# Asking for the inputs of units 8 to 11 as soon as their buffers are free

## The chip, the cores and the metric

One core of a Trainium2 chip runs the kernel. The metric is device time in microseconds (us); of several executions the median is given. Beside it stands one execution that was taken with the profiler.

## What is computed

The kernel joins a gated scan over 4 sequences of 3648 tokens (256 channels) with a two-level mixture of experts: a router picks one of 4 groups and one of 4 experts in it for each of the 14592 tokens, so one of 16 experts, each a two-layer network of 256 to 1024 to 256.

```
sig = 1 / (1 + exp(-f_logit));  f = lower_bound + (1 - lower_bound) * sig
for t in range(S):  h = f[:, t] * h + (1 - f[:, t]) * x[:, t];  y[:, t] = h
x = y.reshape(B * S, D)
g = argmax(x @ w_group);  e = argmax(x @ w_expert[g]);  weights g_w, e_w by softmax
out[token] = g_w * e_w * (relu(x[token] @ w1[g, e]) @ w2[g, e])
```

## The kernel before

**Units.** The tokens are cut into 29 units of 512. Each unit's input (gate and x, 1 MB) is fetched by `p1_load` (L178 to L203). Units 4 to 7 land in eight 512 KB staging tiles `st`; all others land in tiles `zt`, of which four exist. So units 0 to 3 take the four, and units 8 to 11 take them again in the same order. Units up to 11 are asked for by SyncE (SP) on its queue, later ones by ScalarE (ACT), L202. A unit then passes tanh (L216) and an affine step (L226) on ScalarE, a gate (L263 or L242) and two scans (L253) on VectorE, a transpose to rows on TensorE (L281) with its copy (L283), the router's matmuls (L300) and the routing on VectorE. GpSimd scatters the rows to per-expert lists in DRAM (`xs`, L390). The last reader of a unit's `zt` is its second scan.

**Jobs.** An expert's rows are worked on as jobs. The first sixteen ("A") begin before all tokens are routed; job n is cut at the unit that `EARLY` names, and `choose` (L644) picks its expert, so that its weights can be fetched. Jobs 0 to 2 are "raw": f32 weights, four pieces of 512 KB straight into tiles `w` (L939), rows into `xr` (L926), first layer L1043 with its evictions to `hh` and `hl` at L1046, second layer L1078 with its eviction at L1109. Later jobs go through `st` (L943) and a split into two 16-bit parts (L951, L953). Rows in front of a list's start are filled from `blank` (L674).

**Order.** SP issues in the order in which the program is written, for the whole kernel. TensorE, VectorE and ScalarE follow the written order only up to the first job's preparation; from there on a planner lays out their order from the program and its dependences. A background queue of steps (`p1_thunks`) carries the units, and jobs run between them. At unit 3 `choose` fetches the weights of job 0 (`fetch_to` at L665). At unit 5 `early_rows(4)` fetches job 0's rows, then unit 8, then the four pieces of job 1, then unit 9. At unit 7 `early_rows(6)` fetches job 1's rows, unit 10, the four pieces of job 2, unit 11:

```python
        if u == EARLY[0][0]:
            p1_load(8)
            fetch_to(pptr[0] + 4)
            p1_load(9)
        if u == EARLY[1][0]:
            p1_load(10)
            fetch_to(pptr[0] + 4)
            p1_load(11)
```

The tanh of unit u + 1 is written into the steps of unit u; that of unit 11 stands in the steps of unit 10, behind the load of unit 12.

Of the kernel before, what the change touches and what calls it, by code (L numbers as in the profile page):

```python
# [44 lines left out]
MT = -(-max(CAPS) // 128)  # L45
QUARTERS = (13, 14, 15)
ZX_SP = 12


@with_exitstack  # L50
def gated_scan_moe(ctx: ExitStack, tc, zx, lower, wroute, wexp, out, S):
# [110 lines left out]
    def unit_range(u):  # L162
        return u * UNIT, min(N, (u + 1) * UNIT)
# [14 lines left out]
    def p1_load(u):  # L178
        if u >= NU or u in loaded:
            return  # L180
        loaded.add(u)
        a, b = unit_range(u)
        w = b - a
        src = zx[u * P:(u + 1) * P, :].rearrange("p (s k w) -> p s k w", s=2, k=KD)
        if u in STAGED:
            halves = []
            for q in range(2):
                t = stg.tile([P, 1024], F32, name="st").rearrange("p (k w) -> p k w", k=KD)
                nc.sync.dma_start(out=t[:, :, 0:w], in_=src[:, q, :, 0:w])
                halves.append(t)  # L190
            units[u] = {"z": halves[0], "x": halves[1]}
            return
        zt = p1.tile([P, 2, KD, UNIT], F32, name="zt", bufs=4)
        if u == 0:
            for k in range(KD):
                for q in range(2):
                    nc.sync.dma_start(out=zt[:, q, k, 0:w], in_=src[:, q, k, 0:w])
        elif u == 1:
            for k in range(KD):
                nc.sync.dma_start(out=zt[:, :, k, 0:w], in_=src[:, :, k, 0:w])  # L200
        else:
            last_load[u] = (nc.sync if u < ZX_SP else nc.scalar).dma_start(out=zt[:, :, :, 0:w], in_=src[:, :, :, 0:w])  # L202
        units[u] = {"z": zt[:, 0], "x": zt[:, 1]}  # L203
# [239 lines left out]
    def p1_thunks(us, groups, parts):  # L443
# [22 lines left out]
        def put(f):  # L466
            th.append(f or (lambda: None))
            if hasattr(f, "mark"):
                marks[f.mark] = len(th)
# [28 lines left out]
        for u in us + [us[-1] + 1]:  # L498
            seq = []
            if u <= FAST:  # L500
                put(lambda u=u: [p1_load(v) for v in range(2, 8 if u < 8 else u + AHEAD)])
                ending = u - 1 in ends
                if not ending:
                    put(lambda u=u: p1_ta(u + 1))
                if u > 0:
                    put(lambda u=u: p1_router(u - 1))
                    put(lambda u=u: logits(u - 1))
                    if u > 1:
                        put(lambda u=u: p1_gate(u))
                put(lambda u=u: p1_tb(u, 0))  # L510
                wave(u, 1)
                if ending:
                    bind, bound, (s1, f4x, s2, f3, f4, s6, f5, s7s) = routing(u - 1)
                    if u - 1 == BEHIND[2]:
                        f4.mark = "ranked"
                    put(bind)
                    if u > BEGIN:
                        back(u - 1)
                    put(lambda u=u: p1_tanh(u + 1))
                    put(s1)  # L520
                    put(f4x)
                    if u > 1 and member[u - 2] == member[u - 1]:
                        back(u - 2)
                    put(s2)
                    put(f3)
                    put(f4)
                    wave(u, 1)
                    put(lambda u=u: p1_affine(u + 1))
                    back(u - 1)
                    put(bound)  # L530
                    put(s6)
                    put(f5)
                    for f in s7s:
                        put(f)
                    wave(u, 1)
                elif u > 7:
                    wave(u, 1)
                    back(u - 1)
                for m in [m for m, v in ROWS_AT.items() if u == v]:
                    f = lambda m=m: early_rows(m)  # L540
                    f.mark = m
                    put(f)
                if u == BEGIN:
                    f = lambda: None
                    f.mark = "first"
                    put(f)
                put(lambda u=u: p1_tb(u, 1))
                wave(u, 1 if u < FAST else 99)
                if u in cuts and u - 1 in ends:
                    put(lambda u=u: place(u))  # L550
                if u - 1 in ends:
                    put(lambda u=u: choose(u))
                if u == FAST:
                    f = lambda: None
                    f.mark = "begun"
                    put(f)
                    for v in [v for v in sorted(cuts) if v <= FAST and v not in ROWS_AT]:
                        f = lambda v=v: early_rows(v)
                        f.mark = v
                        put(f)  # L560
                continue
            if u in us:
                seq += [lambda u=u: (p1_load(u + AHEAD - 1), u + 1 in us and p1_ta(u + 1))]
            if u - 1 in us:
                seq += [lambda u=u: p1_back(u - 1, 0)]
            if u in us:
                seq += [lambda u=u: p1_tb(u, 0)]
            if u - 1 in us:
                seq += [lambda u=u: p1_router(u - 1)]
                seq += [lambda u=u: p1_back(u - 1, 1)]  # L570
            if u in us:
                seq += [lambda u=u: p1_tb(u, 1)]
            if u - 1 in us:
                seq += [lambda u=u: logits(u - 1)]
            for t in seq:
                put(t)
                slot += 1
                for _ in range(1):
                    if not hold:
                        break  # L580
                    f = hold.popleft()
                    if isinstance(f, tuple) and f[0] == "scat":
                        scatq.extend((slot + n, g) for n, g in zip(PACE, f[1]))
                    elif isinstance(f, tuple):
                        lagq.append((slot + LAG, f[1]))
                    else:
                        put(f)
                while scatq and scatq[0][0] <= slot:
                    put(scatq.popleft()[1])
                while lagq and lagq[0][0] <= slot:  # L590
                    put(lagq.popleft()[1])
            if u - 1 in ends:
                grp = ends[u - 1]
                T = sum(unit_range(v)[1] - unit_range(v)[0] for v in grp) // P
                G = {}

                def bind(G=G, first=grp[0]):
                    G.update(cur.pop("G"))
                    G["rows"] = group_rows.pop(first)
                if u <= 13:  # L600
                    s1, f4x, s2, f3, f4, s6, f5, s7s = route_thunks(G, T, True)
                    rs = [s1, s2, f3, f4x, None, f4, s6, f5]
                else:
                    s1, s2, s3, s4, s5, s6, s7s = route_thunks(G, T)
                    rs = [s1, s2, s3, None, None, s4, s5, s6]
                rs.append(("scat", s7s))
                put(bind)
                rs.append(lambda u=u: choose(u))
                if u in cuts:
                    rs.append(lambda u=u: place(u))  # L610
                    f = lambda u=u: early_rows(u)
                    f.mark = u
                    rs.append(("lag", f))
                hold.extend(rs)
# [77 lines left out]
    def early_rows(u):  # L692
        for mac in macros:
            for j in mac:
                if j.kind == "A" and EARLY[j.idx][0] == u and j.idx < NE - 1:
                    job_rows(j)
        ready[0] = True
        if u == EARLY[0][0]:
            p1_load(8)
            fetch_to(pptr[0] + 4)  # L700
            p1_load(9)
        if u == EARLY[1][0]:
            p1_load(10)
            fetch_to(pptr[0] + 4)
            p1_load(11)

    regs = {}
    early_loads = []
# [423 lines left out]
    pptr = [0]  # L1132
# [28 lines left out]
    def fetch_to(n):  # L1161
        while pptr[0] < min(n, len(pieces)):
            j, i = pieces[pptr[0]]
            if j.kind == "A" and j.idx not in picked:
                return
            if j.kind != "A":
                bg_to(marks["order"])
            job_weights(j, i)
            pptr[0] += 1
        if ready[0]:  # L1170
            ready[0] = False
            blanks()
# [158 lines left out]
```

## Time and profile before

| | us |
|---|---|
| median of 3 runs (766.83 to 768.5) | 767.49 |
| the profiled execution, whole | 772.1 |
| its span, first to last instruction | 770.3 |
| TensorE (PE) busy in the span | 720.9 |
| VectorE (DVE) busy | 530.1 |
| ScalarE (ACT) busy | 450.3 |
| mean granted TensorE clock, share of full | 0.983 |

The profiled execution is 0.6% longer than the median, and 1.8 us of it lie outside the span. The rows below show one execution: starts are us from the span's start; "idle before" with an arrow tells how long an engine stood and what released it. PE and DVE are in the page's words TensorE and VectorE, SPq and ACTq the instructions by which SyncE and ScalarE start a transfer. A busy PE is not a PE at its peak.

### The profile page before, as it was taken

The numbers are of one execution on the slowest core, as the hardware profiler recorded it, in microseconds if no ns is written. First come the engines' busy times: TensorE is split into PE (matmuls) and PEld (weight loads), VectorE is DVE, ScalarE is ACT, GpSimd is POOL, SyncE is SP. The second block draws the span as 40 slices with busy tenths as digits, with TensorE's granted clock in tenths as the row PEclk, the third lists the DMA queues.
The fourth block names the chain that finished last, engine by engine and source line by source line (L and its number), as shares of the span: only waits on it lengthen the run. The fifth ranks groups of instructions, "written<-read, shape, count | busy, mean of one in ns | idle before, by whom it ended". The sixth has DMA issues, their size and how long they took to land.

```text
span 770.3 us, 21391 instructions
## 1 busy us (share of the span) xinstructions
PE 720.9 (94%) x8115; PEld 640.5 (83%) x8115; DVE 530.1 (69%) x1155; ACT 450.3 (58%) x824; POOL 294.5 (38%) x273
## 2 busy tenths in 40 slices
PE   3669799999999999999999999999999999999995
PEld 1557587788878888998999889999999999999995
DVE  6997279999999996678647555454653665657652
ACT  6657368879776965555546444444544555556652
POOL 3666145367775564551221122213322232223223
PEclk9969899999999999999999999999999999999998
DMA  8688899898899666377868652334263555566521
GB/s 325 225 276 314 287 291 323 307 366 289 290 328 320 208 200 212 85 202 185 195 175 183 155 138 83 99 102 124 84 148 111 158 141 162 142 189 182 180 78 32
DMA packets 101383, 152.00 MB, mean 197 GB/s; under 512 B 60898, under 2 KB 70913, under 8 KB 98464
## 3 DMA queue, kind: packets, MB, share of 16 engines
q1 hardware_dynamic: 86752, 103.27, 46.7%
q0 software_dynamic: 11408, 30.02, 10.7%
q10 hardware_dynamic: 3120, 17.34, 6.5%
q8 instruction: 64, 1.05, 0.6%
q14 instruction: 39, 0.32, 0.1%
HBM read 112.66 MB, written 38.40 MB: 196 GB/s over the span
## 4 chain that ended last, share of the span: by engine, by line
PE 66%; DVE 13%; DMA 10%; issue 5%; ACT 3%; POOL 2%; SPq 1%; POOLq 0%; DVEq 0%; ACTq 0%
PE ps_m L1097 31%; PE ps_m L1065 7%; PE ps_m L1067 7%; PE ps_m L1066 7%; DMA zt<-in_zx_dram 3%; PE ps_p L1065 3%; PE ps_p L1066 3%; PE ps_p L1067 3%; DVE h L253 3%; DMA xs<-rows,posi 2%; DVE w L953 2%; PE ps_p L281 2%; DVE hl L1071 2%; DMA st<-in_wexp_dram 2%; ACT zt L226 1%
## 5 line engine op out<-in xcount | busy, mean ns | idle before, releaser
L1097 PE MATMUL ps_m<-w,hh 128*128 128x256 bf16 (+7 forms) x2480 | 304.5, 251 | 0.1
L1097 PE MATMUL ps_m<-w,hl 128*128 128x256 f16 (+3 forms) x1240 | 250.3, 251 | 0.0
L1097 PEld LDWEIGHTS <-hh 128*128 128x128 f16 (+4 forms) x2480 | 183.1, 99 | 21.2 <-issue 2.7
L1065 PE MATMUL ps_m<-xh,w 128*128 128x256 f16 (+10 forms) x782 | 187.2, 254 | 5.4 <-DVE hl L1071 5.4
L1066 PE MATMUL ps_m<-xl,w 128*128 128x256 bf16 (+10 forms) x782 | 187.1, 254 | 0.0
L1067 PE MATMUL ps_m<-xh,w 128*128 128x256 f16 (+10 forms) x782 | 187.1, 254 | 0.0
L390 POOL DMA_INDIRECT xs<-rows,posi x114 | 138.0, 1210 | 121.2 <-ACT rows L285 26.1
L953 DVE TENSOR_TENSOR w<-st,w 128x1024 bf16<-128x1024 f32 x116 | 140.0, 1219 | 50.3 <-ACT w L951 50.3
L1111 POOL DMA_INDIRECT out_dram<-o,info x71 | 83.7, 1178 | 233.4 <-ACT o L1109 204.3
L1071 DVE SCALAR_TENSOR_TENSOR hl<-ps_m,hh 128x512 bf16<-128x512 f32 (+9 forms) x166 | 109.8, 667 | 57.8 <-ACT hh L1070 57.5
L1070 ACT ACTIVATE hh<-ps_m 128x512 f16<-128x512 f32 (+9 forms) x166 | 97.4, 588 | 66.2 <-PE ps_m L1067 66.0
L951 ACT CAST w<-st 128x1024 f16<-128x1024 f32 x116 | 120.2, 1051 | 13.3 <-PE ps_m L1097 8.4
L1066 PEld LDWEIGHTS <-w 128*128 128x128 f16 x1088 | 106.4, 98 | 11.6 <-issue 4.6
L1065 PEld LDWEIGHTS <-w 128*128 128x128 f16 x1088 | 106.5, 98 | 8.4 <-issue 1.2
L1067 PEld LDWEIGHTS <-w 128*128 128x128 bf16 x1088 | 106.4, 98 | 7.0 <-issue 0.2
L1097 PEld LDWEIGHTS <-hl 128*128 128x128 bf16 (+3 forms) x1240 | 97.7, 99 | 11.6 <-issue 2.2
L1111 POOL DMA_INDIRECT out_dram<-o,meta x51 | 59.7, 1171 | 107.0 <-ACT o L1109 94.5
L1109 ACT ACTIVATE o<-ps_m,info 128x256 f32<-128x256 f32 (+4 forms) x71 | 31.5, 444 | 75.0 <-PE ps_m L1097 66.9
L1065 PE MATMUL ps_p<-xh,w 128*128 128x256 f16 (+17 forms) x306 | 71.5, 249 | 0.0
L1066 PE MATMUL ps_p<-xl,w 128*128 128x256 bf16 (+17 forms) x306 | 71.5, 249 | 0.0
L1067 PE MATMUL ps_p<-xh,w 128*128 128x256 f16 (+17 forms) x306 | 71.5, 249 | 0.0
L1071 DVE SCALAR_TENSOR_TENSOR hl<-ps_p,hh 128x512 bf16<-128x512 f32 (+13 forms) x65 | 41.8, 644 | 42.4 <-ACT hh L1070 42.1
(179 smaller groups left out, 827.7 us busy)
## 6 DMA issues: line engine op xcount, KB each, us to landing
st<-in_wexp_dram SPq DMA_DIRECT2D x116, 512.0 KB, 6.5
zt<-in_zx_dram ACTq DMA_DIRECT2D x16, 1024.0 KB, 8.0
xs<-blank SPq DMA_DIRECT2D x28, 258.0 KB, 6.0
zt<-in_zx_dram SPq DMA_DIRECT2D x6, 1024.0 KB, 14.4
w<-in_wexp_dram SPq DMA_DIRECT2D x12, 512.0 KB, 12.8
st<-in_zx_dram SPq DMA_DIRECT2D x8, 512.0 KB, 13.6
xr<-xs SPq DMA_DIRECT2D x14, 258.0 KB, 3.2
xs<-rows,posi POOLq DMA_INDIRECT x114, 6.6
```

The source lines that it names most:

```text
L253: sn = nc.vector.tensor_tensor_scan(out=h[:, k, c0 - a:c1 - a], data0=ff[:, k, c0 - a:c1 - a], data1=uu[:, k, c0 - a:c1 - a], initial=init ...
L390: sc = nc.gpsimd.indirect_dma_start(out=xs_v[G["t0"] + t][:, :], out_offset=bass.IndirectOffsetOnAxis(ap=R["posi"][:, t:t + 1], axis=0), i ...
L951: nc.scalar.copy(j.wh[i], j.st[i])
L953: nc.vector.tensor_tensor(out=j.wl[i], in0=j.st[i], in1=j.wh[i], op=ALU.subtract)
L1065: nc.tensor.matmul(po, w1_at(j.wh, k, c), xh[:, k], start=(k == 0), stop=False)
L1066: nc.tensor.matmul(po, w1_at(j.wh, k, c), xl[:, k], start=False, stop=False)
L1067: nc.tensor.matmul(po, w1_at(j.wl, k, c), xh[:, k], start=False, stop=(k == KD - 1))
L1070: eviction[0] = nc.scalar.activation(hi, pv, AF.Relu).ins
L1071: nc.vector.scalar_tensor_tensor(out=j.hl[ch][:, cs[0]:cs[-1] + 1, 0:w], in0=pv, scalar=0.0, in1=hi, op0=ALU.max, op1=ALU.subtract)
L1097: nc.tensor.matmul(pm[i * q:i * q + n, 0:dw], h[ch][:, c, ts], w2_at(w, c)[:, i * dw:(i + 1) * dw], start=(c == 0 and s == 0), stop=(c == ...
L1109: nc.scalar.activation(o[s, 0:dw], pm[s, 0:dw], AF.Copy, scale=lt.bitcast(F32)[s, r, 1:2])
L1111: nc.gpsimd.indirect_dma_start(out=out_v[out_n[0]].rearrange("n (g d) -> (n g) d", g=g), out_offset=bass.IndirectOffsetOnAxis(ap=lt[s, r, ...
```

## The change

Units 8 to 11 are asked for in other places of SP's order. Unit 8 comes with the steps at the head of unit 2, units 9 and 10 with those at the head of unit 3, unit 11 behind unit 3's second scan and ahead of `choose`, which is to say ahead of job 0's weights. The four loads in `early_rows` go away; the two fetches of job weights there stay. Each load still waits for its buffer. Nothing else changes: the same transfers, the same tiles, the same arithmetic.

```diff
+NEXT_AT = {2: (8,), 3: (9, 10)}
+LAST_AT = {3: (11,)}
...
                 put(lambda u=u: [p1_load(v) for v in range(2, 8 if u < 8 else u + AHEAD)])
+                put(lambda u=u: [p1_load(v) for v in NEXT_AT.get(u, ())])
...
                 if u - 1 in ends:
+                    put(lambda u=u: [p1_load(v) for v in LAST_AT.get(u, ())])
                     put(lambda u=u: choose(u))
...
-        if u == EARLY[0][0]:
-            p1_load(8)
+        if u in (EARLY[0][0], EARLY[1][0]):
             fetch_to(pptr[0] + 4)
-            p1_load(9)
-        if u == EARLY[1][0]:
-            p1_load(10)
-            fetch_to(pptr[0] + 4)
-            p1_load(11)
```

## Rows read from the trace of the kernel before

**Rows 1.** The page, part 2: 40 slices of 19.3 us, busy tenths.
```profile
PE   3669799999999999999999999999999999999995
DMA  8688899898899666377868652334263555566521
```

**Rows 2.** Windows: span, PE, PEld, DVE, ACT, POOL busy us (count), clock, DMA share, GB/s.
```profile
80.00:90.00 10.00, 7.11 (x50) 5.58 (x48) 0.00 (x0) 1.02 (x2) 0.97 (x1) 1.00 0.97 370
94.00:96.00 2.00, 2.00 (x8) 1.63 (x7) 1.90 (x2) 1.76 (x5) 0.00 (x0) 0.50 0.34 117
```

**Rows 3.** ScalarE in order of time: start, us, line, instruction, idle before and releaser.
```profile
76.91 0.33 ACTq L202 DMA_DIRECT2D zt<-in_zx_dram  x1
80.80 0.59 ACT L283 COPY rows<-ps_p 128x512 f32<-128x512 f32 x1
...
90.91 1.06 ACT L216 ACTIVATE zt<-zt 128x1024 f32<-128x1024 f32 x1 [9.53 <-DMA zt<-in_zx_dram]
91.87 0.58 ACT L1046 ACTIVATE hh<-ps_m 128x512 f32<-128x512 f32 x1
...
94.38 1.07 ACT L216 ACTIVATE zt<-zt 128x1024 f32<-128x1024 f32 x1
```

**Rows 4.** TensorE in order of time, across the stall.
```profile
86.51 0.59 PE L1043 MATMUL ps_m<-xl,w 128*128 128x256 f32 x2
92.50 1.22 PE L1043 MATMUL ps_m<-xh,w 128*128 128x256 f32 x2 [5.40 <-ACT hh L1046]
...
98.46 0.69 PE L281 MATMUL ps_p<-ident,h 128*128 128x128 f32 x4
```

**Rows 5.** VectorE in order of time, across the stall.
```profile
93.89 1.23 DVE L242 SCALAR_TENSOR_TENSOR zt<-zt 128x1024 f32<-128x1024 f32 x1 [14.43 <-ACT zt L226]
```

**Rows 6.** SP's transfers in order of time.
```profile
5.39 10.42 SPq L189 DMA_DIRECT2D st<-in_zx_dram  x8
33.44 2.35 SPq L939 DMA_DIRECT2D w<-in_wexp_dram  x4
...
47.62 0.37 SPq L202 DMA_DIRECT2D zt<-in_zx_dram  x1
...
66.08 0.91 SPq L926 DMA_DIRECT2D xr<-xs  x2
...
71.09 0.48 SPq L202 DMA_DIRECT2D zt<-in_zx_dram  x1
```

**Rows 7.** Line 202, both queues, 0 to 160 us: time from issue to landing.
```profile
DMA to landing us min/median/max: 6.0/8.2/14.4
```

**Rows 8.** Windows from 24 to 90 us, columns as in the second group.
```profile
24.00:34.00 10.00, 7.25 (x63) 5.24 (x56) 8.91 (x25) 6.41 (x15) 8.00 (x7) 1.00 0.45 166
34.00:44.00 10.00, 5.68 (x54) 4.62 (x54) 8.82 (x31) 4.72 (x12) 5.72 (x5) 1.00 0.89 281
44.00:48.00 4.00, 3.15 (x29) 2.25 (x28) 3.79 (x12) 2.78 (x7) 0.98 (x2) 0.50 0.17 58
48.00:67.00 19.00, 15.96 (x116) 13.14 (x117) 16.51 (x52) 12.61 (x30) 11.78 (x11) 0.75 0.91 308
```

**Rows 9.** VectorE in order of time: second scan of unit 3.
```profile
29.12 1.25 DVE L253 TENSOR_TENSOR_SCAN h<-zt,h 128x512 f32<-128x512 f32 x1
```

**Rows 10.** TensorE in order of time: job 0's first matmuls, job 1's row transposes.
```profile
57.38 0.82 PE L1043 MATMUL ps_m<-xh,w 128*128 128x256 f32 x2
...
69.07 0.36 PE L1009 MATMUL ps_p<-ident,xr 128*128 128x128 f32 x1 [0.94 <-DMA xr<-xs]
69.70 0.63 PE L1009 MATMUL ps_p<-ident,xr 128*128 128x128 f32 x3 [0.28 <-DMA xr<-xs]
```

**Rows 11.** Windows from 100 to 300 us, and the sum of all four.
```profile
100.00:130.00 30.00, 28.45 (x210) 23.59 (x209) 23.45 (x62) 21.53 (x44) 15.83 (x14) 1.00 0.94 341
130.00:160.00 30.00, 27.18 (x295) 23.44 (x294) 29.72 (x62) 22.69 (x42) 14.52 (x12) 1.00 0.91 309
...
sum 200.00, PE 191.96 PEld 167.20 DVE 185.76 ACT 152.97 POOL 121.42; mean PE 47.99 PEld 41.80 DVE 46.44 ACT 38.24 POOL 30.36
```

## The prediction, made blind
> **What bounds the kernel now.** I began with the page's forty slices [rows 1]. From the sixth slice on TensorE is at 9 tenths nearly throughout, with one hole in the fifth (77 to 96 us) in which the transfer engines stay at 8; so the end is set by TensorE's work, and only time that TensorE loses can be won. The windows show the hole: from 80 to 90 us VectorE does nothing, ScalarE is busy 1.02 us, and the transfer share is 0.97 [rows 2]. A whole core waits for data.
>
> For what, ScalarE's order of time tells. After a row copy at 80.80 it stands 9.53 us until 90.91, released by a `zt` transfer, and then does a tanh [rows 3]. SP's order of time names the transfer: the last `zt` load of SP, unit 11, issued at 71.09 [rows 6]. So 1 MB took 19.8 us, where the loads of this line take 8.2 us in the middle and 14.4 at most among those whose landing is listed [rows 7]. Behind the tanh, in ScalarE's order, stands the eviction of job 1's first layer at 91.87 [rows 3]. TensorE waits for that eviction, 5.40 us, and when it starts at 92.50 it runs at half speed: the two matmuls that take 0.59 us at 86.51 take 1.22 and the granted clock is 0.50, the 1.2 GHz level of the two [rows 2, 4]. VectorE stood 14.43 us for the same unit [rows 5]. This is the only place where the input of a unit holds up all engines.
>
> **What the change removes.** Unit 11 is now asked for as soon as unit 3's second scan ends: that scan starts at 29.12 and takes 1.25, so about 30.5 us instead of 71.09 [rows 6, 9]. Units 8 to 10 go before it. Even at the longest listed landing of 14.4 us [rows 7] unit 11 is there at 45, some 35 us before ScalarE comes to it. The 9.53 us vanish wholly; the working is which part of it TensorE gets.
>
> - TensorE's wait for the eviction: 5.40 us [rows 4].
> - The half clock behind it. From 92.50 to 98.46 TensorE works 5.96 us, at 0.50 [rows 2, 4]. If it hasn't stood, the clock stays at 1.00 as it was until then, and the same work takes half: 3.0 us. Bounds: 0, if TensorE stops elsewhere nearby and the clock falls all the same, and 3.0. I take 3.0, because the busy stretch ahead of the stall ran at full clock.
> - Job 1's rows. TensorE waits 0.94 and 0.28 us for `xr`, issued at 66.08 [rows 6, 10]. SP holds that issue until the scatters have landed, and from 48 to 67 us the transfer engines are at 0.91 with units 8 and 9 and job 1's weights among their load [rows 8]. Without the two units some 2.1 MB are gone from it, 5.7 us of full share at 370 GB/s (166 GB/s at a share of 0.45). I take all 1.2 us; the bounds are 0 and 1.2.
>
> The sum is 5.4 + 3.0 + 1.2 = 9.6 us, with bounds 5.4 and 9.6 from these three terms.
>
> **What it adds: the same four loads, earlier.** No instruction is new; four issues of some 0.4 us each move on SP's queue [rows 6]. Each waits for its buffer, and SP stands meanwhile. Behind them are only the blank rows and job 0's weights, issued at 33.44 [rows 6]; these need `choose`, which comes on VectorE after unit 3's scan, the very thing unit 11's load waits for. So the wait costs nothing and the issue some 0.4 us. SP is free from 15.8 us on, when it has issued the staged halves [rows 6].
>
> What is dearer is what they carry past: 4.19 MB ahead of job 0's weights on one queue. At 370 GB/s that is 11.3 us of all transfer engines. The share is 0.45 from 24 to 34, 0.89 from 34 to 44 and 0.17 from 44 to 48 [rows 8], so 5.5, 1.1 and 3.3 us are free. Job 0's weights are in by about 44 us now, where the share drops. With 11.3 - 5.5 - 1.1 = 4.7 us more ahead they land at about 48.7; if nothing of the free time could be used, at 55.3. Their first matmul starts at 57.38 [rows 10]. Hence nothing is lost, with 2 us to spare in the worst case. The scatters of units 1 to 3 run beside it; their slower landing would hold job 0's row load, which has some 7 us in hand, so 0. In exchange the stretch from 66 to 91 us gets rid of 2.1 MB.
>
> **What is late next.** Once unit 11 is there, ScalarE's next input is unit 12, asked for on its own queue at 76.91 [rows 3]. Its tanh stands at 94.38 now and would stand at about 94.4 - 9.5 - 1.2 = 83.7. With the middle landing of 8.2 us, from 75.7 (the issue moves up by the 1.2), unit 12 is in at 83.9: just in time, 0.2 us or nothing. Job 2's four pieces of weights are the only large load left beside it. From 130 to 160 us VectorE is busy 29.72 of 30 us [rows 11]; it is the bound there, but its own standstill is 14.43 us long [rows 5], so it moves up by no less than TensorE. From 300 us on nothing but TensorE's order counts, and an earlier start is an earlier end.
>
> So 9.6 - 0.1 = 9.5 us. Against the profiled execution that is a span of 760.8 and a whole of 762.6; the median lies 4.6 us under the profile, and 767.49 - 9.5 = **758.0 us**.
>
> **The rivals.**
>
> *Unit 12 takes the place of unit 11.* If its landing takes the 14.4 us of the longest one [rows 7], it arrives at 90.1, and ScalarE stands 6.4 us with the same eviction behind it: 9.5 - 6.4 = 3.1 us remain, 764.4 us. For it: the share is 0.97 now in that window [rows 2]. Against it: unit 11 itself is one of the loads that fill it. There is a rule that bears on this: the Trainium skill, "DMA: Bandwidth & Descriptors", section "Queues, rings and completion order", says that each transfer engine takes turns among the queues that have work for it, a packet from each. By that rule unit 11 lost half its speed when unit 12 started on the other queue, and unit 12 will share with job 2's weights; the trace agrees so far as the 19.8 us go, and the rule pulls toward this rival's 764.4 only if these weights are not yet in at 76.
>
> *The stall is covered by later ones.* Between 100 and 300 us TensorE stands 200 - 192.0 = 8.0 us, with VectorE and the transfers (0.94, 0.91) heavily loaded [rows 11]. If the later pieces of weights and scatters come no earlier, TensorE waits there for what it has won: no change, 767.5. Against it: 4 MB less has to be moved after 48 us. The change not doing what it says falls in here too: SP would have to be held past 60 us.
>
> *The planner's order turns out worse.* Behind job 0's preparation the order of three engines is laid out anew, with unit 11 ready far sooner. If its tanh and scans are put ahead of job evictions, TensorE waits for those. Place: the stretch from 100 to 300 us; price: a scan of 1.25 us [rows 9] for each eviction that falls behind one; point: from 9 such evictions on (9.5 + 1.5 us) the kernel is slower than before. With 16, the price is 20 us and the time 778. For it: VectorE is full there. Against it: the written order and all dependences stay. Job 0's weights being late is no rival of this sign, for they would have to come after 68 us.
>
> *More than the sum.* The 130 to 160 window has 2.8 us of standing TensorE and the one ahead of it 1.6 [rows 11]; with the transfers ahead of their users both could shrink: at most 4.4 us more, 753.6.
>
> **How the numbers follow.** Forecast (755.5 to 761.5): 0.56. More than the sum: 0.10. Unit 12 late, or another part of the 9.5 lost (761.5 to 766): 0.18. No change: 0.09. Worse order: 0.07. The predicted time is the first. The range takes in the first three, and leaves out the last two: 753.0 to 766.0. A measurement of this kernel can tell about 0.2%, 1.5 us, from no change; faster by more than that is 0.84, within it 0.09, slower 0.07.
>
> **What would show it.** SP's order: three `zt` loads between 15.8 and 25 us, one near 30.5, none at 47 to 72. The windows: the share from 24 to 34 near 1, VectorE busy from 80 to 90, no window with a granted clock of 0.50 between 88 and 98. ScalarE: no wait for `zt` of over 2 us behind 60 us; TensorE: the first matmul of job 0 still near 57.4, and the work that stands at 98.46 now near 89. I am wrong if ScalarE stands for unit 12 with evictions behind it, if job 0's first matmul moves, or if TensorE's idle time from 100 to 300 us grows from 8 us by what the stall has lost.

## The result, and the profile after

The changed kernel takes 761.76 us in the median of 6 runs (759.69 to 762.94), beside 768.39 for the kernel before (6 runs, 766.83 to 772.61): a ratio of 0.990, interval 0.988 to 0.992, which is 6 to 9 us. The prediction was 758.0 us, a gain of 9.5; the measured median lies in its range (753.0 to 766.0), but 0.3 us above the forecast's own part of it (755.5 to 761.5), in the part that had a chance of 0.18. The profiled executions stand further apart: 772.1 before and 760.23 after, spans of 770.3 and 758.4, 11.9 us. Lines of the changed kernel below are its own; L204, L218, L924, L937, L941, L1007 and L1107 are the old L202, L216, L926, L939, L943, L1009 and L1109.

The page's slices of the changed kernel answer to [rows 1]:

```profile
PE   3669999999999999999999999999999999999995
DMA  8988899998897854567885752424354455566521
```

TensorE's hole in the fifth slice is filled. Its windows, with the columns of [rows 2] and [rows 8]:

```profile
80.00:90.00 10.00, 10.00 (x88) 8.13 (x88) 6.55 (x15) 8.91 (x20) 0.97 (x1) 1.00 0.73 223
88.00:98.00 10.00, 10.00 (x72) 8.50 (x72) 7.49 (x24) 6.13 (x15) 5.65 (x6) 1.00 1.00 273
...
24.00:34.00 10.00, 7.20 (x63) 5.23 (x56) 8.92 (x25) 6.37 (x15) 7.96 (x7) 1.00 1.03 409
34.00:44.00 10.00, 5.75 (x54) 4.69 (x54) 8.82 (x31) 4.75 (x12) 5.76 (x5) 1.00 1.01 367
44.00:48.00 4.00, 3.16 (x29) 2.24 (x28) 3.79 (x12) 2.76 (x7) 0.98 (x2) 0.51 0.64 252
48.00:67.00 19.00, 15.98 (x114) 12.49 (x115) 17.16 (x51) 15.08 (x33) 11.74 (x11) 0.74 0.69 218
```

VectorE's 0.00 from 80 to 90 has become 6.55, no clock below 1.00 is left between 88 and 98, the transfer share has gone from 0.45 to 1.03 in the 24 to 34 window and from 0.91 to 0.69 between 48 and 67. SP's transfers in order of time, beside [rows 6]:

```profile
16.80 13.92 SPq L204 DMA_DIRECT2D zt<-in_zx_dram  x4
32.71 0.37 SPq L678 DMA_DIRECT2D xs<-blank  x1
33.28 1.98 SPq L937 DMA_DIRECT2D w<-in_wexp_dram  x4
48.31 0.89 SPq L924 DMA_DIRECT2D xr<-xs  x2
...
63.66 0.90 SPq L924 DMA_DIRECT2D xr<-xs  x2
...
82.00 3.56 SPq L924 DMA_DIRECT2D xr<-xs  x4
88.22 1.49 SPq L678 DMA_DIRECT2D xs<-blank  x2
89.97 9.21 SPq L941 DMA_DIRECT2D st<-in_wexp_dram  x7
```

Four loads go out between 16.8 and 30.7 us, job 0's weights at 33.28 instead of 33.44. The rows of job 2 (`xr`, the group of four) are asked for at 82.00; in the kernel before it was 88.76:

```profile
88.76 3.35 SPq L926 DMA_DIRECT2D xr<-xs  x4
93.97 1.46 SPq L674 DMA_DIRECT2D xs<-blank  x2
95.72 27.22 SPq L943 DMA_DIRECT2D st<-in_wexp_dram  x11
```

The prediction did not speak of this line, and the experiments turn on it. What SP waited for ahead of it, between 66 and 90 us, is in the first two lines for the kernel before and in the third for the changed one:

```profile
SPq L926 <- DMA xs<-rows,posi: 8.6, 3, 6.5
SPq L926 <- DMA xs<-blank: 5.9, 1, 5.9
...
SPq L924 <- DMA xs<-rows,posi: 8.8, 3, 7.1
```

(The numbers are the us in total, how often, and the longest.) Job 2's rows can be fetched when the scatters of unit 7 and the blank rows in front of them have landed. In the kernel before the blank rows came last: they are issued behind the four pieces of job 2's weights, land 17.3 us after that, and cost 5.9 us beyond the scatters. In the changed kernel that last wait is gone. From 260 us on the shift between the two kernels does not move any more: the same outputs' evictions on ScalarE start at 271.67 and 714.80 before (first fence), and at 259.78 and 702.92 after (second).

```profile
271.67 0.52 ACT L1109 ACTIVATE o<-ps_m,meta 128x256 f32<-128x256 f32 x1
...
714.80 0.47 ACT L1109 ACTIVATE o<-ps_m,info 128x256 f32<-128x256 f32 x1 [0.49 <-PE ps_m L1097]
```

```profile
259.78 0.52 ACT L1107 ACTIVATE o<-ps_m,meta 128x256 f32<-128x256 f32 x1
...
702.92 0.47 ACT L1107 ACTIVATE o<-ps_m,info 128x256 f32<-128x256 f32 x1 [0.49 <-PE ps_m L1095]
```

So all 11.9 us of the profiled pair arise ahead of the first of these evictions, and none is given back.

### The profile page after: what moved, and what is told of

Its sections match the earlier page's. It is cut to its first block, busy times and chain, and to the rows that moved or that the text cites. A ratio compares the mean times of both kernels' runs of the same rounds, so it can differ in the third digit from the quotient of the medians.

```text
span 758.4 us, 21398 instructions
## 1 busy us (share of the span) xinstructions
PE 718.3 (95%) x8115; PEld 638.5 (84%) x8115; DVE 531.1 (70%) x1155; ACT 450.3 (59%) x824; POOL 296.0 (39%) x273
## 4 chain that ended last, share of the span: by engine, by line
PE 62%; DVE 19%; DMA 8%; issue 4%; ACT 3%; SPq 1%; POOL 1%; POOLq 0%; ACTq 0%; DVEq 0%
PE ps_m L1095 30%; PE ps_m L1063 6%; PE ps_m L1065 6%; PE ps_m L1064 6%; DVE h L255 4%; DVE w L951 4%; PE ps_p L1063 3%; DMA st<-in_wexp_dram 3%; PE ps_p L1065 3%; PE ps_p L1064 3%; DVE hl L1069 3%; DMA xs<-rows,posi 3%; PE ps_p L283 1%; DVE zt L244 1%; ACT w L949 1%
## 5 line engine op out<-in xcount | busy, mean ns | idle before, releaser
L392 POOL DMA_INDIRECT xs<-rows,posi x114 | 141.1, 1238 | 111.3 <-ACT rows L287 25.6
L1109 POOL DMA_INDIRECT out_dram<-o,info x71 | 83.7, 1179 | 233.2 <-ACT o L1107 203.1
L1109 POOL DMA_INDIRECT out_dram<-o,meta x51 | 59.9, 1175 | 104.8 <-ACT o L1107 93.7
L1107 ACT ACTIVATE o<-ps_m,info 128x256 f32<-128x256 f32 (+4 forms) x71 | 31.6, 445 | 73.6 <-PE ps_m L1095 65.8
```

Source lines behind the costliest of these rows:

```text
L392: sc = nc.gpsimd.indirect_dma_start(out=xs_v[G["t0"] + t][:, :], out_offset=bass.IndirectOffsetOnAxis(ap=R["posi"][:, t:t + 1], axis=0), i ...
L1107: nc.scalar.activation(o[s, 0:dw], pm[s, 0:dw], AF.Copy, scale=lt.bitcast(F32)[s, r, 1:2])
L1109: nc.gpsimd.indirect_dma_start(out=out_v[out_n[0]].rearrange("n (g d) -> (n g) d", g=g), out_offset=bass.IndirectOffsetOnAxis(ap=lt[s, r, ...
```

## The experiments

Twelve kernels ran in three groups of four, each group beside the kernel before on one chip. The level differs between the groups: the kernel before took 788.89, 796.3 and 768.97 us there. So ratios to it are compared, and times of different groups are not. Three theories were held: **L**, the gain is unit 11's landing; **T**, it is the 4 MB that leave the crowded stretch; and, formed after the first two groups, **C**, two chains end together near 90 us, unit 11's input and, on SP, job 2's rows with job 3's weights behind them, and both have to come sooner. Line numbers are each kernel's own.

The profiled executions don't all begin alike. Unit 5's tanh stands at 32.3 to 32.7 us in the pair above and in the third group, and at 34.8 to 37.4 in the first two, also in kernels whose moved line comes only later. So starts of a few us apart can't be compared between these, and the third group is the cleanest.

**The kernel before once more (first group).** No edit.

> The kernel before, unchanged, profiled once more. Theory S (the stall for unit 11 is not equally long in every execution, and the profiled one had a long one: its span was 4.6 us over the median's): the wait of ScalarE for unit 11 is shorter here than 9.5 us, some 5 to 7, TensorE's wait 1 to 4 us, and the span shorter by as much. Rival R (the stall is always the same and the executions differ elsewhere, for instance in TensorE's clock or in the stretch from 100 to 270 us): the wait is again 9 to 10 us and TensorE's 5.4, whatever the span is. Time: 767 to 770 us by both.

Ratio 1.0009 (0.998 to 1.004). ScalarE, TensorE and the clock at the stall:

```profile
93.19 1.06 ACT L216 ACTIVATE zt<-zt 128x1024 f32<-128x1024 f32 x1 [7.59 <-DMA zt<-in_zx_dram]
...
94.78 1.22 PE L1043 MATMUL ps_m<-xh,w 128*128 128x256 f32 x2 [3.47 <-ACT hh L1046]
...
94.00:96.00 2.00, 1.22 (x3) 1.04 (x4) 0.00 (x0) 2.00 (x4) 0.00 (x0) 0.59 0.14 49
96.00:98.00 2.00, 2.00 (x9) 1.53 (x8) 1.73 (x2) 1.78 (x5) 0.00 (x0) 0.56 0.04 12
98.00:100.00 2.00, 2.00 (x27) 1.53 (x26) 2.00 (x3) 2.00 (x5) 0.00 (x0) 1.00 0.75 245
```

The stall is there again and smaller: 7.59 instead of 9.53 us on ScalarE, 3.47 instead of 5.40 on TensorE, and the clock is back at 98 us, after some 3.4 us at half, where it stayed low for 6.8 before. Theory S (the text above has it, and its rival R) is right that the stall has no fixed length, and wrong that a shorter one goes with a shorter span: this execution had a span of 795.0 where the median whole time was 790. What the stall cost in the median execution stays open.

**Unit 11 alone in its old place (first group).**

```diff
-LAST_AT = {3: (11,)}
+LAST_AT = {}
...
         if u in (EARLY[0][0], EARLY[1][0]):
             fetch_to(pptr[0] + 4)
+        if u == EARLY[1][0]:
+            p1_load(11)
```

> Units 8, 9 and 10 asked for early as in the change, unit 11 alone in its old place behind job 2's weights. Theory L (the gain is unit 11's landing, and a load asked for at 71 us behind 2 MB of weights lands too late whatever else is gone): ScalarE still waits for unit 11, some 4 to 8 us, and the time is 763.5 to 768. Rival T (the gain is the relief of the transfer engines, 3 of the 4 MB are gone from the crowded stretch): unit 11 lands in some 10 us, the wait is under 2 us and the time 761 to 763.

Ratio 0.9964 (0.993 to 0.999). In this execution ScalarE did not wait for unit 11 at all: it stood for a second-layer matmul until 86.17 and went straight on to the tanh, which by T should have been worth most of the gain. It was not: the time is in L's band, the wait in T's. Job 2's rows were asked for at 89.33, but TensorE does not wait for them: from 72 to 100 us it never stands, and its clock is 1.00. This execution was behind earlier (job 0's first matmul at 62.12, in the kernel before of this group at 57.49), and later ScalarE waits 3.02 us for unit 14's input:

```profile
110.05 1.06 ACT L218 ACTIVATE zt<-zt 128x1024 f32<-128x1024 f32 x1 [3.02 <-DMA zt<-in_zx_dram]
```

Neither theory holds as it was put.

**Unit 11 ahead of job 2's weights (first group).** The kernel before, one line moved.

```diff
             p1_load(10)
+            p1_load(11)
             fetch_to(pptr[0] + 4)
-            p1_load(11)
```

> The kernel before with one line moved: unit 11 is asked for directly behind unit 10 at unit 7, ahead of job 2's weights instead of behind them (67.5 instead of 71.1 us). Units 8 to 10 stay where they were. Theory L: unit 11 lands in some 6 to 9 us, by 76, the wait is gone and most of the gain is there: 760 to 763. Rival T: nothing is relieved, the same 4 MB go in the same stretch, job 2's weights and the blank rows come 2.5 us later: 766 to 769.

Ratio 1.0037 (1.0003 to 1.007): not faster. Yet ScalarE's waits for `zt` between 57 and 140 us are gone and the tanh of unit 12 comes at 89.94, against 96.7 in the kernel before in this group. So unit 11's wait was taken away and nothing was won; L falls. SP shows what became later instead:

```profile
93.86 2.97 SPq L926 DMA_DIRECT2D xr<-xs  x4
100.14 1.46 SPq L674 DMA_DIRECT2D xs<-blank  x2
102.15 18.81 SPq L943 DMA_DIRECT2D st<-in_wexp_dram  x11
...
118.30 1.04 ACT L951 CAST w<-st 128x1024 f16<-128x1024 f32 x1 [2.10 <-DMA st<-in_wexp_dram]
...
121.45 0.74 PE L1009 MATMUL ps_p<-ident,xr 128*128 128x128 f32 x4 [1.81 <-ACT rows L283]
```

Against the kernel before in this group, job 2's rows went from 89.57 to 93.86 and job 3's weights from 98.32 to 102.15. Of these 4.3 us, 2.6 stood there already at job 1's rows (69.33 instead of 66.74), ahead of the moved line. The rest goes with the blank rows, behind one more megabyte: for them SP waits last, 3.5 us, where in the kernel before of this group it was the scatters. TensorE waited only 0.30 us for the rows themselves; the loss came through what lies behind them. At unit 12's tanh this execution is 6.7 us ahead of the kernel before, at unit 15's only 1.3 (123.00 and 124.28). In between ScalarE stands three times for job 3's weights, 3.2 us in all, and TensorE 1.81 us behind it; at 134.59 it stands another 2.00 us for the rows of a later job.

**Unit 11 behind job 0's weights (first group).** The change, two lines exchanged.

```diff
-                    put(lambda u=u: [p1_load(v) for v in LAST_AT.get(u, ())])
                     put(lambda u=u: choose(u))
+                    put(lambda u=u: [p1_load(v) for v in LAST_AT.get(u, ())])
```

> The changed kernel with unit 11 asked for directly behind job 0's weights instead of in front of them (36 instead of 30.4 us). Theory L: unit 11 is there by 50, 30 us before it is needed, so nothing changes: within 0.2% of the changed kernel, 760.5 to 763, and job 0's weights land 2 to 3 us sooner without effect. Rival F (being in front of the first job's weights does harm, as the first matmul of job 0 came at 57.97 instead of 57.38): 0.5 to 1.5 us faster than the changed kernel.

Ratio 0.9901 (0.986 to 0.994): the changed kernel's. Job 2's rows were asked for at 85.11, 4.5 us sooner than in the kernel before in this group. To stand in front of the first job's weights brings nothing and costs nothing that can be measured.

**The changed kernel once more (second group).** No edit.

> The changed kernel, unchanged, as the mark for the three runs beside it: ratio to the kernel before 0.988 to 0.993. Both theories say the same here.

Ratio 0.9878 (0.984 to 0.991); job 2's rows at 83.95.

**Copies in the old places (second group).** The changed kernel with the same bytes moved again, once in all four places and once in the last two.

```diff
+    spare = nc.dram_tensor("spare", [4 * P, zx.shape[1]], F32).ap()
+    def again(u):
+        sync.dma_start(out=spare[(u - 8) * P:(u - 7) * P, :], in_=zx[u * P:(u + 1) * P, :])
...
+            again(8)
             fetch_to(pptr[0] + 4)
+            again(9)
```

> The changed kernel, and in each of the four old places of the loads a copy of the same 1 MB of input from DRAM to a spare place in DRAM, in the same shape, read by nobody. Units 8 to 11 are there early, but the transfer engines are not relieved between 47 and 91 us. Theory L (the gain is that ScalarE, VectorE and TensorE no longer wait for unit 11): the wait stays away and most of the gain stays, ratio 0.988 to 0.994. Theory T (the gain is that SP's later transfers, the blank rows, job 2's rows and job 3's weights, come sooner once the 4 MB are gone from that stretch): job 2's rows are asked for at 88 to 94 us as in the kernel before, and the ratio is 0.997 to 1.006.

> As the run with four copies, but with copies only in the old places of units 10 and 11, around job 2's weights. Theory L: ratio 0.988 to 0.993. Theory T, if the last 2 MB are what holds the blank rows back: ratio 0.996 to 1.004; if the first 2 MB count as much, half the gain, 0.993 to 0.997.

Ratios 1.0109 (1.007 to 1.015) and 1.0013 (0.998 to 1.004). The numbers fall on T's side, but the test is not clean: the copies were no stand-in for the loads. With four of them SP itself stood 26.0 us, in two waits, before it could issue a copy, so job 1's rows were asked for at 86.28 instead of 65.84, and TensorE waited for them:

```profile
SPq L699 <- DMA zt<-in_zx_dram: 26.0, 2, 21.0
...
91.82 0.46 PE L1018 MATMUL ps_p<-ident,xr 128*128 128x128 f32 x1 [12.42 <-DMA xr<-xs]
```

They show that a delay in SP's order reaches TensorE through the rows of a job; of the 4 MB they tell nothing.

**Unit 11 late but ahead of job 2's weights (second group).** Units 8 to 10 early.

```diff
-LAST_AT = {3: (11,)}
+LAST_AT = {}
...
+        if u == EARLY[1][0]:
+            p1_load(11)
         if u in (EARLY[0][0], EARLY[1][0]):
             fetch_to(pptr[0] + 4)
```

> Units 8 to 10 early, unit 11 at unit 7 directly ahead of job 2's weights, so that it lands by 73 to 76 us, in time, while 3 of the 4 MB are gone from the crowded stretch. Theory L: the full gain, 0.988 to 0.992. Theory T: job 2's weights and the blank rows come some 2.5 us later than in the changed kernel, so three quarters of the gain or less: 0.993 to 0.997.

Ratio 0.9945 (0.991 to 0.998), where the changed kernel has 0.9878 in the same group. ScalarE waits for no input. Job 2's rows come at 87.89 instead of 83.95, job 3's weights at 95.41 instead of 91.33:

```profile
87.89 2.97 SPq L926 DMA_DIRECT2D xr<-xs  x4
93.68 1.47 SPq L678 DMA_DIRECT2D xs<-blank  x2
95.41 11.48 SPq L943 DMA_DIRECT2D st<-in_wexp_dram  x8
...
62.39 1.22 PE L1043 MATMUL ps_m<-xh,w 128*128 128x256 f32 x2 [2.06 <-issue]
```

With unit 11 in time in both, 4 us on SP's chain go with 0.7% of the time, about 5 us. That the one causes the other is not shown. SP waits here for the scatters, not for the blank rows, and the last scatter itself was issued 5.8 us later (83.47 instead of 77.66). TensorE stands at job 0's first matmul (last line; 0.42 us in the changed kernel), and from 60 to 72 us its clock is 0.58 on the mean instead of 1.00. From 72 to 100 us it does not stand at all. So this execution lost its time before the moved load, asked for at 66.50, could matter; whether the other eight did is not known.

**Both chains by order alone (third group).** The kernel before; no byte leaves the crowded stretch.

```diff
             p1_load(10)
+            p1_load(11)
+            blanks()
             fetch_to(pptr[0] + 4)
-            p1_load(11)
```

> The kernel before, with only the order at unit 7 changed: job 1's rows, unit 10, unit 11, the blank rows, and then job 2's weights. No byte leaves the crowded stretch. Theory C (two chains end together near 90 us: unit 11's input, and on SP the blank rows, job 2's rows and job 3's weights behind them; the time follows the later one): unit 11 lands by 78, job 2's rows are asked for at 82 to 87 instead of 89 to 94, and the ratio is 0.988 to 0.996. Theory T (what counts is that 4 MB leave the stretch): 0.998 to 1.004, as when only unit 11 was moved ahead. Theory L (unit 11 alone) has fallen already, by that run.

Ratio 0.9945 (0.992 to 0.997): half of the gain, and against the run that moved unit 11 alone (1.0037, in the first group) one more line made the difference. Job 2's rows are at 82.56. Theory C's band holds, T's does not. What is still missing is seen where [rows 10] had 0.94 and 0.28: the rows of job 1, which nothing relieves here, are waited for longer.

```profile
68.43 0.36 PE L1010 MATMUL ps_p<-ident,xr 128*128 128x128 f32 x1 [0.40 <-DMA xr<-xs]
70.42 0.92 PE L1010 MATMUL ps_p<-ident,xr 128*128 128x128 f32 x3 [1.63 <-DMA xr<-xs]
```

With 1.08 us for VectorE at 67.76, TensorE stands 43 - 39.90 = 3.1 us from 57 to 100 us, all of it here, and the clock is at 0.50 for some 3.4 us behind it. In the changed kernel it stands 0.1 us; the two spans, 761.6 and 758.4, are 3.2 us apart.

**SP's chain alone (third group).** Units 8 to 10 early, unit 11 behind job 2's weights, blank rows in front of them.

```diff
         if u in (EARLY[0][0], EARLY[1][0]):
+            if u == EARLY[1][0]:
+                blanks()
             fetch_to(pptr[0] + 4)
+        if u == EARLY[1][0]:
+            p1_load(11)
```

> Units 8 to 10 early, unit 11 behind job 2's weights as in the first run of that kind, and the blank rows ahead of these weights instead of behind them. Theory C: job 2's rows move up to 83 to 86 us, unit 11's wait of some 3 us stays; the ratio goes from 0.996 to 0.989 to 0.994. Theory T: no byte moves, the ratio stays at 0.994 to 0.999.

Ratio 0.9972 (0.995 to 1.000): C's number was missed. The rows did come at 83.61, but the wait of 3 us that I had put to unit 11 was a misreading: in the first run of that kind it was unit 14's, and unit 11 had none. Here unit 11's is nearly 6 us; TensorE stands 1.91 us at 88.09 for the eviction behind it, and the clock falls:

```profile
86.50 1.06 ACT L218 ACTIVATE zt<-zt 128x1024 f32<-128x1024 f32 x1 [5.95 <-DMA zt<-in_zx_dram]
...
90.00:92.00 2.00, 2.00 (x22) 1.25 (x20) 1.90 (x2) 2.00 (x5) 0.00 (x0) 0.50 0.28 88
92.00:94.00 2.00, 2.00 (x7) 1.71 (x8) 1.97 (x6) 2.00 (x6) 0.00 (x0) 0.50 0.67 191
```

The size was wrong, the mechanism shows: with job 2's rows early, it is unit 11 that holds the kernel.

**The changed kernel with the blank rows first (third group).**

```diff
         if u in (EARLY[0][0], EARLY[1][0]):
+            if u == EARLY[1][0]:
+                blanks()
             fetch_to(pptr[0] + 4)
```

> The changed kernel with the blank rows of jobs 2 and 3 ahead of job 2's weights. Theory C: job 2's rows come 1 to 4 us sooner, held then by unit 7's scatters alone; if this chain is still the later one, the ratio to the kernel before is 0.983 to 0.988, a little better than the changed kernel's 0.988 to 0.990. If not, 0.988 to 0.991.

Ratio 0.9907 (0.988 to 0.993), job 2's rows at 81.99, not sooner than the 82.00 of the changed kernel, so that part of the expectation was missed. In both kernels SP waits for unit 7's scatters (6.5 us here and 8.8 in the changed kernel, in three waits each): the blank rows are no longer the last to arrive.

**Job 3's weights earlier (third group).** The changed kernel.

```diff
-            fetch_to(pptr[0] + 4)
+            fetch_to(pptr[0] + (4 if u == EARLY[0][0] else 8))
```

> The changed kernel, with job 3's four pieces of weights asked for at unit 7 directly behind job 2's, at about 67 to 70 us instead of 90 to 94. Theory C in its narrow form (the end of SP's chain, job 3's weights, is what binds): ratio 0.980 to 0.987. If it is job 2's rows that bind, these come later behind 2 MB more: 0.990 to 1.000.

Ratio 0.9978 (0.996 to 1.000): nearly the whole gain is lost, though unit 11 is there early and ScalarE waits for no input. So the narrow form, that job 3's weights bind, falls. Job 2's rows are at 90.04, SP having waited 7.0 us for the blank rows behind 2 MB more, and now TensorE waits for them:

```profile
90.04 3.38 SPq L924 DMA_DIRECT2D xr<-xs  x4
...
92.25 0.41 PE L1007 MATMUL ps_p<-ident,xr 128*128 128x128 f32 x1 [4.44 <-DMA xr<-xs]
93.15 0.91 PE L1007 MATMUL ps_p<-ident,xr 128*128 128x128 f32 x3 [0.49 <-DMA xr<-xs]
...
94.00:96.00 2.00, 2.00 (x14) 1.70 (x14) 0.43 (x3) 0.77 (x4) 0.00 (x0) 0.50 0.36 85
```

This is the plainest of the twelve: 4.9 us of standing TensorE and the half clock after it, at the place and of the size of unit 11's stall, made by the other chain.

The runs side by side (the copies left out). The fourth column tells what SP waited for last ahead of job 2's rows, the fifth TensorE's longest stand between 72 and 100 us, if it was 0.3 us or more. All but the ratio come from one execution each.

| kernel | ScalarE's wait for unit 11, us | job 2's rows asked for, us | SP's last wait | TensorE stands, us | ratio |
|---|---|---|---|---|---|
| before, profiled / once more | 9.53 / 7.59 | 88.76 / 89.57 | blank rows / scatters | 5.40 / 3.47 | 1 / 1.0009 |
| 8 to 10 early, 11 behind job 2's weights | none | 89.33 | scatters | none | 0.9964 |
| 11 ahead of job 2's weights | none | 93.86 | blank rows | 0.30 | 1.0037 |
| changed, job 3's weights earlier | none | 90.04 | blank rows | 4.44 | 0.9978 |
| 8 to 10 early, blank rows first, 11 behind | 5.95 | 83.61 | scatters | 1.91 | 0.9972 |
| 8 to 10 early, 11 ahead of job 2's weights | none | 87.89 | scatters | none | 0.9945 |
| order alone: 11 and blank rows first | none | 82.56 | scatters, blank rows | none | 0.9945 |
| changed, 11 behind job 0's weights | none | 85.11 | scatters | none | 0.9901 |
| changed, blank rows first | none | 81.99 | scatters | none | 0.9907 |
| changed (two measurements) | none | 82.00 / 83.95 | scatters | none | 0.990 / 0.9878 |

Two runs of the third group make one chain late by itself: unit 11 (0.9972) and job 2's rows (0.9978). Each brings TensorE's stand and the half clock back and takes most of the gain away. With both early the ratio is near 0.99 where the four units are early, and 0.9945 by order alone. So theory C holds for the place of the stall. It does not explain all: where units 8 to 10 are early and unit 11 late but in time (0.9964 and 0.9945), TensorE stands for neither chain, and why these gain less is not shown.

One rival was not separated. In every kernel with all four units early ScalarE does unit 8's tanh at 49.7 to 55.6 us, in all others at 59.1 to 66.5, also where unit 8 was asked for as early. So the planner's order of the engines differs between the two kinds, and part of the difference between 0.9945 and 0.99 may come from that. It is not the whole gain, for the kernel with job 3's weights earlier has that order too and 0.9978. No version was measurably better than the changed kernel.

## Why the prediction was right, and where not

- **The stall as the place** was right: the hole of [rows 2] is gone, and both TensorE's wait and the half clock with it. From 57 to 100 us TensorE stood 43 - 35.91 = 7.1 us before and 43 - 42.86 = 0.1 after. These 7.0 us are the 5.4 and 1.2 of the sum and 0.4 besides. But unit 11 was only one of two chains that end there, as the point on what is late next tells.
- **The half clock**, 3.0 us, was right for the profiled pair: no 0.50 is left between 88 and 98.
- **More than the sum** came true in that pair. Between 100 and 300 us TensorE stood 8.0 us before [rows 11] and 200 - 194.3 = 5.7 after, 2.3 less. With 7.0 + 3.0 + 2.3 = 12.3 the 11.9 us of the two spans are accounted for within 0.4.
- **The step that was mis-sized** is the one from the profiled execution to the median. I subtracted 9.5 us from the median as if each execution lost as much. But the profiled execution lay 3.7 us above the median of six, the changed kernel's 1.5 below its own, and 11.9 - 3.7 - 1.5 = 6.7 is what the medians show (6.6; this is arithmetic, and names no cause). The second profile of the kernel before has the terms at 3.47 instead of 5.40 and at some 1.7 (half of 3.4) instead of 3.0; their sum is 5.2, not 8.4. That was in another group, at another level, so it shows that the terms vary, and not that the median loses exactly this.
- **"What is late next" was incomplete.** It looked at unit 12 alone and found it in time; it was (its tanh stands at 82.76 with no wait for data). It did not look at SP's rows of job 2 and what lies behind them, which would have been late next: with unit 11 repaired and these at 90 us or later the gain is 0.2% or none. The gain came through because the same change brought them from 88.76 to 82.00, as SP no longer waited 5.9 us for the blank rows. I had counted the relief of that stretch at 1.2 us, for job 1's rows. That the sum came near the profiled pair was luck in this: the second chain moved by about as much, and the sum would have promised nearly the same for the kernels that won nothing.
- **The rivals.** Unit 12 in unit 11's place did not happen. The Trainium skill's turn-taking among queues ("DMA: Bandwidth & Descriptors", section "Queues, rings and completion order") pulled toward it. Unit 12's tanh waits for no data in the changed kernel, so no run here shows the rule at work; nor do unit 11's 19.8 us, since 2 MB of job 2's weights stood ahead of it on its own queue. Covered by later stalls: not in the changed kernel, but it is what befell two variants in which unit 11 was no longer waited for (11 ahead of job 2's weights, job 3's weights earlier; 1.0037 and 0.9978). The planner's order did change (the first matmul of job 0 stands at 57.97 instead of 57.38, with the router's matmuls in front of part of the row transposes; unit 8's tanh at 49.90 instead of 59.74), without the loss that this rival named. "If job 0's first matmul moves" was a sign of being wrong; the 0.6 us are within what executions differ by, 57.24 and 58.37 in two other kernels with the four units early.
- **What it adds**, at nothing: right. Job 0's weights were early enough even behind 4 MB, and putting unit 11 behind them gave the same ratio.

## What to carry to other kernels

When a stall has one clear releaser, follow every other chain that feeds the same engine through the same moment before booking the stall as gain; a second input a few us later can take the whole gain. Look at small loads that queue behind large ones: here 129 KB of blank rows behind 2 MB of weights held the rows of a whole job, and to have them sooner was as necessary as the transfer that the stall named. Where executions begin differently, compare what TensorE stood for, and not only when a transfer was asked for. And of a stall that depends on contention one profile gives one length: take a second one before its size goes into a sum.

## What the runs showed of the hardware

- The kernel before took 788.89, 796.3 and 768.97 us in the three groups. The granted clock of its profiled execution was 0.983 ahead of the prediction and 0.965 in the first group, where from 160 to 200 us it was 0.87 on the mean instead of 1.00. Why the groups differ was not tried.
- The clock fell to 0.50 (the 1.2 GHz level) around the end of a stand of TensorE of 5.40 us and stayed there for some 6.8 us, around one of 3.47 us for some 3.4 us (both in the kernel before), and behind one of 1.91 us and a further one of 0.42 us for some 6.8 us (blank rows first, 11 behind). The times at 0.50 are worked out from the clocks of windows of 2 us. A shorter stand did not mean a shorter time at half clock.
- Blank rows of 129 KB, issued at 70.07 us behind 2 MB of weights, landed 17.3 us later in the kernel before.
- With copies of 1 MB from DRAM to DRAM among its issues SP stood 26.0 us in two places before it could issue a copy, where the issue of a load of the same shape into the core took it some 0.4 us. The trace names the landing of an input tile as what released it; what held SP there was not tried.
